# Attention steps in groups of four scores, two-bank maxima, a held GpSimd queue and re-placed norm rows in a transformer block

## The chip, the cores and the metric

The kernel runs on one core of one Trainium2 chip. The metric is device microseconds of that core for one execution. A kernel's time is the median of its runs. Engines are named as in the profile: PE (TensorE), DVE (VectorE), ACT (ScalarE), POOL (GpSimd), SP (SyncE); PEld is PE's loading of weights.

## The reference

One block with a conditioning vector: softmax attention with 32 heads of 16 dimensions over 2048 tokens, then a gated feed-forward part, in float32.

```python
mod = (silu(c) @ w_mod).reshape(1, 6, 1, 512); sa, ca, ga, sb, cb, gb = mod[:, 0..5]
h = layernorm(x) * (1 + ca) + sa                       # x: 1 x 2048 x 512
q, k, v = split_heads(h @ wqkv)                        # 32 heads of 16
p = softmax(q @ k.T * 16 ** -0.5)                      # 32 x 2048 x 2048
x = x + ga * (merge(p @ v) @ wo)
h = layernorm(x) * (1 + cb) + sb
x = x + gb * ((silu(h @ w_gate) * (h @ w_up)) @ w_down)    # 512 -> 1792 -> 512
```

## The kernel before

**Units and steps.** Attention is cut into 32 units of 4 heads by 512 queries. A unit takes 16 steps of 128 keys, so there are 512 steps. Eight units make a chunk of 512 tokens; there are four chunks, and the output projection and the feed-forward part of a chunk follow its attention, mixed into the attention of the next chunk.

**What a step issues.** For each of its four heads a pair of matmuls: `score` (L506) for the present step and `max_one` (L479) for the step 19 steps ahead, whose result only serves to find each query's maximum. The two use opposite halves of PE's rows and run side by side. ACT reads a score from its PSUM bank and writes its exponential (L508). DVE reduces the max matmul's bank to one maximum for each of 128 queries (L481). Then come the products with V (L521): two "halves" of a step, each of four matmuls of 256 columns; they may use a step's exponentials once the following step's four pairs have been issued. `pair_of` issues a pair, `pvs` the products with V, `close_unit` what follows a unit's last product (copy of the result `o` by ACT, L525; the softmax denominators go through DRAM and come back as `rb`; `out_c` multiplies on POOL and stores).

**Banks.** PSUM has eight banks of 512 columns. In steps without filler (`plain`) the max matmuls rotate over banks 0 to 3 (`four`), the scores over banks 4, 5 and 6 (`bank`), and the products with V accumulate in bank 7 (`single`). Every engine works its instructions in the order of issue; the whole order is written out by hand, and a matmul into a bank waits until the reader of that bank's last contents is done.

**Where steps are plain, where filled.** `plain(n)` runs n steps of attention alone, `filled` runs pairs with matmuls of the output projection or of the feed-forward part between them. `plain` takes the first 147 steps (the first chunk has nothing to mix in), then in each of the three chunks 12 steps while the chunk's rows are normed and transposed (`turned`, four of them, "tails"), 3 steps before the last `down` in two chunks, 21 steps at two chunk starts and 24 (`REST`) in the third: 255 of the 512 steps. In `plain` before, a group is three pairs (`WIN`) and then two, one, one, two halves of products (`HALVES`), so three steps make four groups.

**Unit ends.** Twelve steps into a unit the maxima of the next one are complete: `max_rows` reduces them on DVE (L486), PE transposes them (L491 to L493) into one of the score banks, ACT copies them to `mr` (L495), and SP's queue writes them into the rows of `qop` that the next unit's scores read (L497, `qop<-mr`).

**POOL.** During the first chunk POOL splits the weights into high and low parts (`split_weights`, three portions in each unit) and stores them to DRAM (`wo_dr`, `gu_dr`, `wd_dr`) through its own DMA queue. Nothing ties these portions to the attention's steps but POOL's order and `out_c`, which waits for `rb`. `begin` makes a chunk's object, loads its rows of x (`load_x2`) and its output weights (`load_wo`) through the same queue.

**The end.** After step 512 PE finishes the seven kept jobs of chunk 2 (`rest`), the last output projection, the norm of the last chunk's rows, their transposes, and the whole feed-forward part of chunk 3, with no attention beside it.

Of the kernel before, what the change touches and what calls it, by code (L numbers as in the profile page):

```python
# [39 lines left out]
WIN = 3  # L40
HALVES = (2, 1, 1, 2)
# [6 lines left out]
NORM = 9  # L48
# [53 lines left out]
def block_kernel(ctx, tc, x, wqkv, wo, w_gate, w_up, w_down, c, w_mod, out):  # L102
# [9 lines left out]
    banks = [ps.tile([P, CW], F32, name=f"bank{i}") for i in range(8)]  # L112
# [340 lines left out]
    posts = []  # L453
    n = 16 * NU
# [15 lines left out]
    def max_one(r):  # L470

        u, t = divmod(r // 4, 16)
        b, e = 1 - r % 4 // 2, r % 2
        s, qt, kc = t // 8, t // 2 % 4, t % 2 * 2 + e
        if u not in mx:
            mx[u] = pb.tile([P, 2, 2, 4, NC], F32, name="mx", tag="mx", bufs=3)
        rows = slice(64 * b, 64 * b + KR)
        pm = four("pm")
        nc.tensor.matmul(pm, qop[u][rows, s, qt * P:(qt + 1) * P], kop[u % 3][rows, s, kc * CW:(kc + 1) * CW],  # L479
                         start=True, stop=True)  # L480
        nc.vector.tensor_reduce(mx[u][:, b, s, qt, kc:kc + 1], pm, op=ALU.max, axis=AX.X)  # L481
# [281 lines left out]
    def gate_up(ch, f, outs, halves):  # L763
# [5 lines left out]
        def after():  # L769
            th = tmp("th")  # L770
            nc.scalar.activation(th, outs[0], AF.Tanh, scale=0.5)  # L771

            def later():
                q = tmp("q")
                nc.vector.scalar_tensor_tensor(q, th, 1.0, outs[0], op0=ALU.add, op1=ALU.mult)  # L775
                m32 = tmp("m32")
                nc.vector.tensor_mul(m32, outs[1], q)  # L777
                (nc.gpsimd.tensor_copy if halves else nc.scalar.copy)(mid[:, 0, :], m32)  # L778
                (nc.gpsimd if halves else nc.vector).tensor_sub(mid[:, 1, :], m32, mid[:, 0, :].bitcast(F32))  # L779
            posts.append(later)  # L780
# [25 lines left out]
    def begin(ci):  # L806
# [5 lines left out]
        ch.load_wo([as_wo(tile_gu()) for _ in range(NK // 2)])  # L812
# [20 lines left out]
    def close_unit(u, i):  # L833
        if u == NU - 1:
            res[u] = out_a(u, nc.scalar)
            return
        res[u] = out_a(u, nc.sync)
# [3 lines left out]
        if u % NG == NG - 1:  # L841
            at(i + 1, lambda: begin(u // NG))
# [9 lines left out]

    weights2 = split_weights()

    def after(i):
# [15 lines left out]
        if 0 <= i < UG and i % 16 in (1, 4, 7):  # L871
            next(weights2, None)
# [13 lines left out]
    done, ended, owed = 0, 0, 0  # L886
# [14 lines left out]
    def pvs(most, by_halves):  # L901

        nonlocal owed
        if by_halves:
            most, owed = most + owed, 0
        while most and halves and 4 * halves[0][0] + 8 <= done:
# [3 lines left out]
            if i % 16 == 15 and half:  # L910
                close_unit(i // 16, done // 4 - 1)
                if by_halves:
                    break
        if by_halves and most and halves and 4 * halves[0][0] + 8 <= done:
            owed = most
# [7 lines left out]
    def plain(steps, tails=()):  # L923

        nonlocal four, bank
        assert steps % WIN == 0 and done % 4 == 0
        four, bank = Turn(0, 1, 2, 3), Turn(4, 5, 6)
        for w in range(4 * steps // WIN):
            for _ in range(WIN):
                pair_of()  # L930
            if w >= 4 * steps // WIN - len(tails):
                tails[w - 4 * steps // WIN](four())
            pvs((HALVES[(w - 2) % 4] if done > 8 else 0) + (w == 4 * steps // WIN - 1), True)
            end_steps()

    def filled(places, work):
# [11 lines left out]
        pvs(6, False)  # L948
# [13 lines left out]
    for ci in range(last):  # L962
# [8 lines left out]
        plain(WIN, [lambda tp, k=k: ch.turned(tp, k) for k in range(NK)])  # L971
        if ci == last - 1:
            plain(REST)
        for _ in range(len(ch.jobs) - (KEEP if ci == last - 1 else 0)):
            job, args = ch.jobs.pop(0)
            if args == (NF // FG - 1, 0):
                plain(WIN)
# [8 lines left out]
    turns = chain([2, 3, 2, 0, 1, 3, 0], cycle([1, 2, 3, 0]))  # L986
# [12 lines left out]
    ch, chp = chunks[last], chunks[last - 1]  # L999
    rest = whole(chp, chp.jobs)  # L1000
# [6 lines left out]
    ch.load_x2(nc.scalar)  # L1007
# [8 lines left out]
    for t in range(4):  # L1016
        ch.normalize(t, True)
# [36 lines left out]
```

## Time and profile before

| | |
|---|---|
| median of 3 runs | 1947.17 us (1943.54 to 1949.21) |
| the profiled execution's own time | 1939.03 us |
| its span, first to last instruction | 1937.2 us |
| PE busy | 1891.8 us (98%) |
| DVE busy | 1551.5 us (80%) |
| ACT busy | 1256.0 us (65%) |
| POOL busy | 378.6 us (20%) |

A row of the profile's groups gives line, engine, operation, tiles as out<-in, shapes and count, then busy time in us and the mean ns of one, then the idle time before them and what ended it. A row of the timeline gives start and length in us, then engine, line and operation; an idle time that ended just there stands in brackets with its releaser. A row of the windows gives the stretch, its length, and each engine's busy time with the count of instructions, then the granted PE clock (1.00 is full), the DMA engines' busy share and GB/s; asked for one line, it counts that line alone. In the chain of waits a row gives start, length and what the chain passed through.

Since PE's records are pipelined (a matmul's record lasts longer than the time until the next may start), a PE that is 98% busy may still wait: the distance between starts tells its pace.

### The profile page before, as it was taken

How to read it: one execution, taken by the hardware profiler on the slowest of the kernel's cores; microseconds unless marked ns; L12 is line 12 of the kernel's file. 1: busy time of each engine (PE TensorE's matmuls, PEld its weight loads, DVE VectorE, ACT ScalarE, POOL GpSimd, SP SyncE). 2: the span in 40 equal slices, each digit the busy share in tenths (PEclk: the TensorE clock that was granted, in tenths of full speed). 3: DMA queues.
4: the chain of work that ended last, by engine and by line, in shares of the span. 5: the costliest groups of instructions: out<-in, count | busy, mean ns of one | idle time of the engine just before them, and what ended most of it. 6: DMA issues, size and time to landing. Idle time of an engine off the chain costs nothing.

```text
span 1937.2 us, 40750 instructions
## 1 busy us (share of the span) xinstructions
PE 1891.8 (98%) x16996; PEld 1152.4 (59%) x16996; DVE 1551.5 (80%) x2562; ACT 1256.0 (65%) x2333; POOL 378.6 (20%) x440
## 2 busy tenths in 40 slices
PE   7999999999999999999999999999999999999999
PEld 5766444444455666666555666666554466666787
DVE  5458999999899888888999888888999988831543
ACT  4222888888787666666777666666778866674211
POOL 3000435543223111111123101111123011121100
PEclk9999999999899999999999999999999999999999
DMA  8764666665453345443444334453532344243543
GB/s 286 274 218 121 185 179 183 194 198 150 141 110 72 103 114 142 138 118 85 133 95 101 100 125 118 122 136 75 153 84 54 97 97 138 111 140 110 222 194 109
DMA packets 79988, 267.60 MB, mean 138 GB/s; under 512 B 17364, under 2 KB 22484, under 8 KB 59124
## 3 DMA queue, kind: packets, MB, share of 16 engines
q1 hardware_dynamic: 64396, 200.22, 37.9%
q0 software_dynamic: 14192, 62.93, 9.4%
q8 instruction: 133, 2.18, 0.5%
q10 hardware_dynamic: 1216, 1.85, 0.3%
q14 instruction: 51, 0.42, 0.1%
HBM read 201.85 MB, written 62.13 MB: 136 GB/s over the span
## 4 chain that ended last, share of the span: by engine, by line
PE 88%; DVE 6%; ACT 3%; DMA 3%; issue 1%; SPq 0%; POOL 0%; ACTq 0%; DVEq 0%; POOLq 0%
PE bank L521 24%; PE bank L506 22%; PE bank L718 19%; PE bank L479 9%; PE bank L209 6%; PE bank L727 6%; DVE x L790 2%; DVE mx L481 2%; DMA qop<-mr 1%; PE bank L491 1%; DVE stt L743 1%; DMA v_flat<-in_A_x 0%; PE bank L703 0%; PE bank L162 0%; DMA wm_ab<-in_w_mod 0%
## 5 line engine op out<-in xcount | busy, mean ns | idle before, releaser
L481 DVE TENSOR_REDUCE mx<-bank 128x1 f32<-128x512 f32 x2048 | 1295.0, 682 | 168.3 <-PE bank L479 108.9
L506 PE MATMUL bank<-qop,kop 50*128 50x512 f32 x2048 | 751.1, 431 | 14.4 <-DMA qop<-mr 8.1
L479 PE MATMUL bank<-kop,qop 48*128 48x512 f32 x2048 | 759.7, 435 | 3.4 <-DVE mx L481 1.9
L506 PEld LDWEIGHTS bank<-qop,kop 50*128 50x128 f32 x2048 | 344.9, 185 | 322.2 <-issue 55.8
L479 PEld LDWEIGHTS bank<-kop,qop 48*128 48x128 f32 x2048 | 342.2, 185 | 29.5 <-DVE mx L481 10.4
L718 PE MATMUL bank<-act,wgu 64*128 64x512 f32 x1872 | 309.1, 394 | 1.5
L718 PEld LDWEIGHTS bank<-act,wgu 64*128 64x128 f32 x1872 | 199.8, 187 | 40.9 <-DVE x L790 9.0
L548 POOL TENSOR_TENSOR on<-o,rb 128x512 f32<-128x512 f32 x31 | 39.8, 1284 | 529.3 <-DMA rb<-d_dr 369.5
L718 PE MATMUL bank<-wd,mid 64*128 64x512 f32 x912 | 140.0, 396 | 1.7
L778 POOL CAST mid<-m 128x512 fp32r<-128x512 f32 x39 | 23.9, 613 | 469.7 <-DVE m L777 469.6
L718 PEld LDWEIGHTS bank<-wd,mid 64*128 64x128 f32 x912 | 92.0, 186 | 26.5 <-DVE x L790 11.0
L209 PE MATMUL bank<-hT,wqs 128*128 128x512 f32 x384 | 97.0, 404 | 3.9 <-DVE prt L369 2.4
L209 PEld LDWEIGHTS bank<-hT,wqs 128*128 128x128 f32 x384 | 71.5, 191 | 26.3 <-issue 5.9
L775 DVE SCALAR_TENSOR_TENSOR q<-th,bank 128x512 f32<-128x512 f32 x56 | 38.1, 680 | 55.8 <-ACT th L771 55.8
L771 ACT ACTIVATE th<-bank 128x512 f32<-128x512 f32 x56 | 33.4, 597 | 58.9 <-PE bank L727 58.5
L790 DVE TENSOR_TENSOR x<-bank,x 128x512 f32<-128x512 f32 x84 | 53.7, 680 | 21.0 <-PE bank L718 21.0
L369 DVE TENSOR_TENSOR prt<-bank,prt 128x512 fp32r<-128x512 f32 x32 | 21.9, 688 | 47.2 <-ACT prt L367 45.2
L367 ACT CAST prt<-bank 128x512 fp32r<-128x512 f32 x32 | 18.8, 586 | 60.5 <-PE bank L209 47.4
L777 DVE TENSOR_TENSOR m<-bank,q 128x512 f32<-128x512 f32 x56 | 38.7, 691 | 22.9 <-PE bank L727 19.2
L727 PE MATMUL bank<-wd,mid 128*128 128x512 f32 x216 | 52.8, 397 | 1.0 <-ACT mid L778 0.6
L779 POOL TENSOR_TENSOR mid<-m,mid 128x512 fp32r<-128x512 f32 x39 | 50.2, 1287 | 3.2
L718 PE MATMUL bank<-wgu,act 64*128 64x512 f32 x288 | 47.9, 395 | 0.1
(6279 smaller groups left out, 5124.5 us busy)
## 6 DMA issues: line engine op xcount, KB each, us to landing
wgu<-gu_dr SPq DMA_DIRECT2D x48, 1024.0 KB
kop<-kd SPq DMA_DIRECT2D x62, 768.0 KB
wd<-wd_dr SPq DMA_DIRECT2D x28, 1024.0 KB
gu_dr<-wgu POOLq DMA_DIRECT2D x14, 1024.0 KB, 4.1
qop<-qd SPq DMA_DIRECT2D x64, 192.0 KB
kd<-prt SPq DMA_DIRECT2D x16, 512.0 KB
qd<-prt SPq DMA_DIRECT2D x16, 512.0 KB
kop<-gu_dr SPq DMA_DIRECT2D x8, 1024.0 KB
```

The costliest lines, as they stand in the source:

```text
L209: nc.tensor.matmul(pt, lhs(a, k), rhs(b, k), start=(n == 0), stop=(n == 3 * nk - 1))
L479: nc.tensor.matmul(pm, qop[u][rows, s, qt * P:(qt + 1) * P], kop[u % 3][rows, s, kc * CW:(kc + 1) * CW], start=True, stop=True)
L481: nc.vector.tensor_reduce(mx[u][:, b, s, qt, kc:kc + 1], pm, op=ALU.max, axis=AX.X)
L506: nc.tensor.matmul(sp, kop[u % 3][rows, h // 2, kt * P:(kt + 1) * P], qop[u][rows, h // 2, :], start=True, stop=True)
L521: nc.tensor.matmul(pv[u][32 * h:32 * h + 32, cols], v_flat[:, e0:e0 + 32], p_[h][:, cols], start=(kt == 0 and half == 0), stop=(kt == 15), ...
L548: mul.tensor_mul(on, o, rb)
L718: nc.tensor.matmul(outs[e], lhs(e, a, k)[rows], rhs(b, k)[rows], start=(ph == 0 and j == 0), stop=(ph == 1 and j == z))
L727: nc.tensor.matmul(outs[e], lhs(e, a, k), rhs(b, k), start=(j == 0), stop=(j == z))
L775: nc.vector.scalar_tensor_tensor(q, th, 1.0, outs[0], op0=ALU.add, op1=ALU.mult)
L777: nc.vector.tensor_mul(m32, outs[1], q)
L779: (nc.gpsimd if halves else nc.vector).tensor_sub(mid[:, 1, :], m32, mid[:, 0, :].bitcast(F32))
L790: nc.vector.tensor_add(ch.x2[:, t, :], outs[e], ch.x2[:, t, :])
```

## The change

1. All eight banks become slices of one PSUM tile `psum`; the banks, their rotation and their waits stay tied to the slices.
2. In `plain` a group is one whole step: four pairs, then up to three halves of products (two are available in a steady row of steps). `WIN`, `HALVES` and the carrying over of owed halves are gone.
3. In `plain` one DVE instruction reduces two neighbouring banks (L485, output 128x2, input 128x2x512) after every second pair, in place of two of 128x512. `filled` steps keep the single reduce.
4. `tails` of `plain` take their bank from the score banks (`bank`) and no longer from the max banks, one per step (four steps, `NK`); the steps before them go from 9 to 8, so the 12 stay 12.
5. In units 0 to 6, `close_unit` queues a copy of one element of `o` to `pin` on POOL (L842), so that POOL goes no further before ACT has written `o`. The first portion of weights in a unit comes after step 2 and no longer after step 1.
6. The first chunk's `begin` moves from its end to step 3; its `load_wo` comes 6 steps after the close of its last unit, not 1, and so behind `out_c`.
7. At the end the last chunk's `load_x2` goes to POOL's queue, right after the last unit is closed, and no longer to ACT's queue behind the chain of `o`; two of its four rows are normed by POOL instead of ACT; its transposes use banks 6 and 7 instead of 4 and 5; the order of banks (`turns`) is changed to suit; and one split of a middle tile (chunk 2, f = 12) goes to POOL.

The core of the diff:

```diff
-WIN = 3
-HALVES = (2, 1, 1, 2)
-NORM = 9
+NORM = 8
-    banks = [ps.tile([P, CW], F32, name=f"bank{i}") for i in range(8)]
+    psum = ps.tile([P, 8, CW], F32, name="psum")
+    banks = [psum[:, i, :] for i in range(8)]
 ...
-        nc.vector.tensor_reduce(mx[u][:, b, s, qt, kc:kc + 1], pm, op=ALU.max, axis=AX.X)
+        if not wide:
+            nc.vector.tensor_reduce(mx[u][:, b, s, qt, kc:kc + 1], pm, op=ALU.max, axis=AX.X)
+        elif e:
+            two = psum[:, r % 4 - 1:r % 4 + 1, :]
+            nc.vector.tensor_reduce(mx[u][:, b, s, qt, kc - 1:kc + 1], two, op=ALU.max, axis=AX.X)
 ...
+        if u < NG - 1:
+            nc.gpsimd.tensor_copy(pin, o_[u][0:1, 0:1])
 ...
-            at(i + 1, lambda: begin(u // NG))
+            if u // NG:
+                at(i + 1, lambda: begin(u // NG))
+            at(i + (1 if u // NG else 6), lambda: chunks[u // NG].load_wo([...]))
 ...
+    at(3, lambda: begin(0))
 ...
     def plain(steps, tails=()):
-        four, bank = Turn(0, 1, 2, 3), Turn(4, 5, 6)
-        for w in range(4 * steps // WIN):
-            for _ in range(WIN):
+        four, bank, wide = Turn(0, 1, 2, 3), Turn(4, 5, 6), True
+        for w in range(steps):
+            for _ in range(4):
                 pair_of()
-            if w >= 4 * steps // WIN - len(tails):
-                tails[w - 4 * steps // WIN](four())
-            pvs((HALVES[(w - 2) % 4] if done > 8 else 0) + (w == 4 * steps // WIN - 1), True)
+            if w >= steps - len(tails):
+                tails[w - steps](bank())
+            pvs(3)
             end_steps()
 ...
+    ch.load_x2(nc.gpsimd)
 ...
-    ch.load_x2(nc.scalar)
 ...
-        ch.normalize(t, True)
+        ch.normalize(t, t < 2)
 ...
-            ch.turned(banks[4 + e], k + e, nc.vector if k else nc.gpsimd)
+            ch.turned(banks[6 + e], k + e, nc.vector if k else nc.gpsimd)
```

What PE has in its queue in a plain row of steps before (bank0 to bank3 take max matmuls, bank4 to bank6 scores, bank7 the products; `qop` and `kop` are a unit's queries and keys, `pt_` the exponentials):

```order
L506 MATMUL bank5_68<-qop_1098,kop1_961 128x512
L479 MATMUL bank0_63<-kop2_1417,qop_1422 128x512
L506 MATMUL bank6_69<-qop_1098,kop1_961 128x512
L479 MATMUL bank1_64<-kop2_1417,qop_1422 128x512
L506 MATMUL bank4_67<-qop_1098,kop1_961 128x512
L479 MATMUL bank2_65<-kop2_1417,qop_1422 128x512
L521 MATMUL bank7_70<-pt__2077,v_flat_88 32x256
L521 MATMUL bank7_70<-pt__2103,v_flat_88 32x256
L521 MATMUL bank7_70<-pt__2082,v_flat_88 32x256
L521 MATMUL bank7_70<-pt__2108,v_flat_88 32x256
L506 MATMUL bank5_68<-qop_1098,kop1_961 128x512
L479 MATMUL bank3_66<-kop2_1417,qop_1422 128x512
```

And at such a place now (the lines of `score` and of the products are 510 and 525 there, and all banks carry the name of the one tile; in the code a score still takes banks 4, 5 and 6 in turn, so the fourth score of a group takes the bank of the first):

```order
L510 MATMUL psum_63<-qop_957,kop0_80 128x512
L479 MATMUL psum_63<-kop1_954,qop_1092 128x512
L510 MATMUL psum_63<-qop_957,kop0_80 128x512
L479 MATMUL psum_63<-kop1_954,qop_1092 128x512
L510 MATMUL psum_63<-qop_957,kop0_80 128x512
L479 MATMUL psum_63<-kop1_954,qop_1092 128x512
L510 MATMUL psum_63<-qop_957,kop0_80 128x512
L479 MATMUL psum_63<-kop1_954,qop_1092 128x512
```

Between two visits to the same score bank there were products with V before; now a group's fourth score follows the first in the same bank with two other pairs between and no product.

POOL at the end of the first chunk before (`gu_dr`, `wd_dr` the stored weights, `x` the rows of x, `on` the multiplied result that waits for `rb`):

```order
L548 TENSOR_TENSOR on<-o,rb 128x512
L549 DMA o_dr<-on 128x512
L621 TENSOR_TENSOR mid<-mid,gb_bc 128x1024
L583 CAST wd<-mid 128x1024
L584 TENSOR_TENSOR wd<-mid,wd 128x1024
L587 DMA wd_dr<-wd 128x2048
L641 DMA x_5478<-in_A_x 128x4x512
L646 DMA wgu<-wo_dr 128x2048 x2
L548 TENSOR_TENSOR on<-o,rb 128x512
```

And now:

```order
L552 TENSOR_TENSOR on<-o,rb 128x512
L553 DMA o_dr<-on 128x512
L625 TENSOR_TENSOR mid<-mid,gb_bc 128x1024
L587 CAST wd<-mid 128x1024
L588 TENSOR_TENSOR wd<-mid,wd 128x1024
L591 DMA wd_dr<-wd 128x2048
L552 TENSOR_TENSOR on<-o,rb 128x512
L553 DMA o_dr<-on 128x512
L650 DMA wgu<-wo_dr 128x2048 x2
```

The load of x has left this place for step 3, and the two loads of output weights stand behind the last unit's multiplication, which waits for that unit's `rb`.

More of the change, by code (lines that the diff above doesn't have):

```diff
@@ L851, in before @@
             load_q(u + 2)
+    at(3, lambda: begin(0))
     weights2 = split_weights()
+    pin = pb.tile([1, 1], F32, name="pin", bufs=1)
     def after(i):
@@ L870, in after @@
             load_q(2)
[L871 removed]
+        if 0 <= i < UG and i % 16 in (2, 4, 7):
             next(weights2, None)
@@ L970, in block_kernel @@
         plain(NORM)
-        plain(WIN, [lambda tp, k=k: ch.turned(tp, k) for k in range(NK)])
+        plain(NK, [lambda tp, k=k: ch.turned(tp, k) for k in range(NK)])
         if ci == last - 1:
@@ L976, in block_kernel @@
             if args == (NF // FG - 1, 0):
-                plain(WIN)
+                plain(3)
             work = job(ch, *args, outs, True)
```

28 lines of the change are left out of this document (12 added, 16 removed).

## The prediction

> **What bounds the kernel now.** I read the page's first and fifth parts, then the windows of the plain stretches, then the timeline inside them, then the chain of waits where a stretch is longer than its pace explains.
>
> ```profile
> PE 1891.8 (98%) x16996; PEld 1152.4 (59%) x16996; DVE 1551.5 (80%) x2562; ACT 1256.0 (65%) x2333; POOL 378.6 (20%) x440
> ...
> L481 DVE TENSOR_REDUCE mx<-bank 128x1 f32<-128x512 f32 x2048 | 1295.0, 682 | 168.3 <-PE bank L479 108.9
> ```
>
> PE looks full everywhere, so the page does not say which engine paces a plain step. The change touches plain steps, so these are counted first: windows over the stretches of `plain`, asked for ACT's exponentials (L508) alone, four of which are a step (588 are 147 steps; a count can lack one).
>
> ```profile
> 189.71:563.42 373.71, 305.65 (x588) 0.98 0.61 169
> 592.28:625.96 33.68, 25.27 (x48) 1.00 0.20 43
> ...
> 940.47:992.47 52.00, 43.70 (x84) 1.00 0.52 142
> ...
> 1483.94:1543.22 59.28, 49.80 (x96) 1.00 0.34 71
> sum 652.67, ACT 530.98; mean ACT 59.00
> ```
>
> All 255 plain steps take 652.67 us, 2.56 each. In a quiet part the pace is DVE's:
>
> ```profile
> 440.55 21.54 DVE L481 TENSOR_REDUCE mx<-bank 128x1 f32<-128x512 f32 x36
> 462.01 0.21 DVE L486 TENSOR_REDUCE m<-mx 128x16 f32<-128x64 f32 x1
> ```
>
> Thirty-six reduces in 21.54 us without a gap are 0.598 us each, four of them 2.39 us: a quiet plain step. The rest, 652.67 - 255 x 2.39 = 43 us, sits at unit ends, tails and stalls. DVE is so the bound of plain steps, and halving its instructions looks like a gain. What would bound next is PE's own order, so I took its distances, start to start, from three pairs followed by two halves of products:
>
> ```profile
> 395.65 0.50 PE L506 MATMUL bank<-qop,kop 50*128 50x512 f32 x1
> ...
> 396.00 0.39 PE L506 MATMUL bank<-qop,kop 50*128 50x512 f32 x1
> ...
> 396.23 0.39 PE L506 MATMUL bank<-qop,kop 50*128 50x512 f32 x1
> ...
> 396.56 0.40 PE L521 MATMUL bank<-pt__3916,v_flat 128*32 128x256 f32 x1
> ...
> 397.56 0.50 PE L506 MATMUL bank<-qop,kop 50*128 50x512 f32 x1
> ```
>
> ```profile
> 396.19 0.60 ACT L508 ACTIVATE pt__3962<-bank 128x512 f32<-128x512 f32 x1
> 396.69 0.59 ACT L508 ACTIVATE pt__3967<-bank 128x512 f32<-128x512 f32 x1
> 397.16 0.60 ACT L508 ACTIVATE pt__3972<-bank 128x512 f32<-128x512 f32 x1
> ```
>
> First pair to second 0.35, second to third 0.23, two halves with both switches 1.00. The first score's exponential starts 0.54 after the score and takes 0.60; later ones follow at 0.47 to 0.50. Three scores, three banks: none waits in its own group.
>
> **The pace of the new group.** The fourth score takes the bank of the first, so it waits for the exponential of a score of its own group, and the products stand behind it in PE's queue. The trace holds this very case once: the last four scores of all rotate over three banks with no filler and no max matmul.
>
> ```profile
> 1766.65 0.73 PE L506 MATMUL bank<-qop,kop 50*128 50x512 f32 x3 [0.23 <-ACT pt__20527 L508]
> 1767.83 0.50 PE L506 MATMUL bank<-qop,kop 50*128 50x512 f32 x1 [0.45 <-ACT pt__20542 L508]
> 1768.26 0.40 PE L521 MATMUL bank<-pt__20504,v_flat 128*32 128x256 f32 x1
> ...
> 1767.18 0.60 ACT L508 ACTIVATE pt__20542<-bank 128x512 f32<-128x512 f32 x1 [0.59 <-PE bank L506]
> ```
>
> Three scores start at 1766.65, the exponential of the first at 1767.18, it ends at 1767.78, the fourth score goes at 1767.83, the products at 1768.26: 1.61 us from first score to products. With 1.00 for two halves and the switch back, the loop is 2.61 us, and it closes: the next group's first score stands behind these products. The other demands are smaller. DVE: 0.68 us for 512 elements and 0.21 for 64 give 1.04 ns per element, so 1024 cost 0.598 + 0.53 = 1.13 a piece, 2.26 a step (bounds: 1.07, no fixed part at all, and 1.36, two records end to end). ACT: four at 0.48, 1.92. The max matmuls add nothing: the second reduce begins about 1.9 after the first score, ends by 3.12, and the third pair that needs its banks comes at 2.61 + 0.58 = 3.19. Up to 1.30 a reduce stays hidden behind the loop, so what the wider reduce saves has no taker. I take 2.61 (bounds 2.55, the fourth score's pair as cheap as a warm one, and 2.72, two reduces of 1.36). 255 steps: 665.6 us.
>
> **Unit ends.** One step with the transposes of the maxima, and the lone transposes of a tail:
>
> ```profile
> 383.58:387.01 3.43, 2.66 (x6) 1.00 0.58 168
> ...
> 616.85 0.66 PE L703 MATMUL bank<-ident,mid 128*128 128x128 f32 x4
> ```
>
> The step costs 3.43 - 2.39 = 1.04 more. In the new group PE idles 1.18 - 0.81 = 0.37 before the fourth score, and the transposes, which stand after the first pair, fall into that: 0.67 is left (bounds 0.3 and 1.04). Of the 255 steps 18 hold one: 12 us.
>
> **Tails.** Four per chunk, twelve in all. Each now holds a score bank: its transposes wait for the second exponential (0.54 + 0.47 + 0.60 + 0.05 = 1.66 after the first score, against 1.61 without) and take 0.66. I take 0.7 each (bounds 0.5 and 1.3, if ACT's copy of that bank delays the next group): 8 us. NORM 8 + 4 keeps the count of steps. The first step has no products yet and saves 1. New sum of the plain stretches: 665.6 + 12 + 8 - 1 = 685, against 652.67: **32 us more**.
>
> **The hold and the moved loads.** The first stretch has 373.71 - 147 x 2.39 = 22 us over pace, 9 of it unit ends. Most of the rest is one place:
>
> ```profile
> 497.67 0.77 POOL L641 DMA_DIRECT2D x<-in_A_x  x1
> 498.44 1.06 POOL L646 DMA_DIRECT2D wgu<-wo_dr  x2
> ...
> 503.77 6.97 DMA qop<-mr
> ...
> 505.00:510.00 5.00, 1.32 (x18) 0.43 (x8) 2.43 (x4) 1.88 (x4) 0.00 (x0) 0.94 0.91 375
> 510.00:515.00 5.00, 4.12 (x24) 1.74 (x24) 1.36 (x3) 1.30 (x3) 0.00 (x0) 0.50 0.02 7
> ...
> 504.71:523.88 19.17, 8.47 (x18) 0.64 0.26 106
> ```
>
> POOL ran ahead of the attention and issued three loads just before the write of `mr`; that took 6.97 us, PE stood still, and its clock fell to 0.50. Four steps took 19.17 instead of 9.6. Both edits, `begin` at step 3 and `load_wo` behind `out_c`, take the loads from there, so these 9.6 and some 3 of smaller stalls go. My 685 already holds none of these 12.5; if the hold fails, they come back. The hold itself I cost at nothing:
>
> ```profile
> POOL on L548 <- DMA rb<-d_dr: 369.5, 20, 37.2
> ```
>
> POOL already waits once a unit for `rb`; now it waits at `pin` first, with the same work behind it. Queued behind are weight portions and `out_c`; nobody needs the weights before step 155, or `on` before the chunk's projection at step 147, some 30 us after the last portion. If that cover went, PE would wait at step 147 by what is late, at most a portion of about 6 us (part of the range). The later `load_wo` has the eleven steps to 147, also covered.
>
> **The end.**
>
> ```profile
> 1784.37 9.05 DMA v_flat<-in_A_x
> 1793.51 1.29 DVE v_flat L739 x2
> ...
> 1792.27 0.69 DVE L779 TENSOR_TENSOR mid<-m,mid 128x512 fp32r<-128x512 f32 x1 [0.69 <-ACT mid L778]
> 1802.01 2.93 ACT L695 ACTIVATE v_flat<-v_flat,rs,rs 128x512 f32<-128x512 f32 x4 [9.28 <-DVE rs L691]
> 1806.92 1.94 PE L703 MATMUL bank<-ident,v_flat 128*128 128x128 f32 x8 [3.08 <-DVE x L790]
> ...
> L698 POOL TENSOR_SCALAR mid<-x,rs,rs 128x512 f32<-128x512 f32 x12 | 9.1, 769 | 0.3
> ```
>
> The earlier load of x frees the additions at 1793.51, but DVE is at L779 until 1792.96: 0.55 won. Two rows on POOL (2 x 0.77) beside two on ACT save 1.4 of 2.93. Banks 6 and 7 no longer wait for L790. So PE's idle 3.08 before the transposes goes nearly whole: 3 us less (bounds 0, if the load of x slows the small transfers of `o`, and 4). The middle tile split on POOL is ready before its `down`: nothing.
>
> **Sum.** 32 - 3 = 29 us. The profiled execution took 1939.03, so 1968; the median of the runs stands 0.42% above it, so **1976 us**, 1.5% slower.
>
> **Rivals.**
>
> *The wait for the fourth score is not paid* (faster). If ACT answered sooner or PE passed the products ahead, the pace would be set by the loop through DVE's banks over two steps: reduce end, third and fourth pair (0.07 + 0.23), products 1.33, second pair 0.35 + 0.44, two reduces 1.13 + 1.21, together 4.76, 2.38 a step. Plain stretches: 255 x 2.38 + 19 = 626, 27 less, with the end 30: 1916 us. It decides from a pace of 2.48 on. The lone group at 1766.65 speaks against it. The Trainium skill, VectorE: DVE Perf Modes, section on the TRN2 errata, says that a fixed latency is paid once per instruction, so that few large tiles beat many small ones; by that alone the change is a gain on DVE. The trace agrees on the fixed part (0.21 for 64 elements, 0.68 for 512), but not that DVE sets the new pace.
>
> *The gains elsewhere cancel it* (no change): pace 2.50 and all stalls gone, about 1947.
>
> *A two-bank reduce costs two records or more* (1.36): DVE paces at 2.72, 28 us on top: 2004. No row shows such a reduce; the slope between 64 and 512 elements speaks against it.
>
> *PE's clock drops* because PE now idles 0.37 in every step. In the stall the clock fell to 0.50 after some 4 us of idling, and at 0.50 a step's four passes of products (4 x 0.22 between 396.56 and the switch) would take twice as long, 3.5 a step: 255 x 0.9 = 230, so 2200. The plain windows with PE's small waits stand at 1.00 throughout, which speaks against it. The Trainium skill, TensorE: Matmul & The Clock Gate, section on a second HAM failure mode, tells of micro-idles between groups of matmuls, as PE cycles through PSUM banks, that throttle the clock; no run here shows it for gaps this short.
>
> **How the numbers follow.** Forecast 0.80, clock 0.02, dear reduce 0.05, cancelled 0.06, wait not paid 0.07. The forecast's own range: pace -15 to +18, unit ends and tails -8 to +14, stalls that stay 0 to +12, end -1 to +3, not all at once: 1956 to 2000. To hold 8 in 10 with the cases beside it: 1950 to 2003. What can be told from no change here is about 0.3% (6 us). Slower 0.88 (forecast, clock, dear reduce, a little of the cancelled), within 0.3% 0.05, faster 0.07.
>
> **What would show it.** In the plain windows: 2.6 us per four exponentials; DVE with gaps, its releaser PE; the fourth score of a group with an idle time released by ACT; two-bank reduces near 1.2 us. At the end of the first chunk no stall of 7 us and the clock at 1.00. Before the last transposes no idle 3 us. Wrong would be: DVE without gaps at 2.3, or plain stretches under 652 us.

## The result and the profile after

The changed kernel takes 1979.4 us (median of 4 runs, 1976.8 to 1980.6) against 1946.9 for the one before (4 runs, 1943.5 to 1949.2): a ratio of 1.017, interval 1.0154 to 1.0185. The forecast was 1976, slower. The profiled execution spans 1975.0 us, 37.8 more than that of before.

First the page of the changed kernel: busy time of PE and DVE, then the group of two-bank maxima, with busy time, mean ns of one, and the idle time before them.

```profile
PE 1912.4 (97%) x16996; PEld 1182.2 (60%) x16996; DVE 1535.2 (78%) x2051; ACT 1254.9 (64%) x2330; POOL 383.4 (19%) x452
...
L485 DVE TENSOR_REDUCE mx<-psum 128x2 f32<-128x1024 f32 x510 | 599.0, 1219 | 80.8 <-PE psum L479 50.7
```

DVE has 511 instructions and 16 us less to do, and idles 80.8 us before its new ones, most of it for want of PE: the saved time found no taker.

The windows over the plain stretches of the changed kernel, exponentials alone (now L512; four are a step, and a window may count the one that closes it):

```profile
191.58:584.06 392.48, 305.58 (x588) 1.00 0.56 161
...
964.53:1020.89 56.36, 43.70 (x84) 1.00 0.48 131
...
sum 692.66, ACT 530.62; mean ACT 58.96
```

Before, the sum was 652.67: **40 us more** for the same 255 steps, in every window. The clock is 1.00 in each of them, so it isn't PE's clock. One quiet step of it, on the timeline of PE and then of ACT; below them a stretch of DVE a few steps on:

```profile
367.93 0.50 PE L510 MATMUL psum<-qop,kop 50*128 50x512 f32 x1
...
368.27 0.40 PE L510 MATMUL psum<-qop,kop 50*128 50x512 f32 x1
...
368.51 0.39 PE L510 MATMUL psum<-qop,kop 50*128 50x512 f32 x1
...
369.12 0.50 PE L510 MATMUL psum<-qop,kop 50*128 50x512 f32 x1 [0.21 <-ACT pt__3325 L512]
...
369.55 0.40 PE L525 MATMUL psum<-pt__3298,v_flat 128*32 128x256 f32 x1
...
370.55 0.50 PE L510 MATMUL psum<-qop,kop 50*128 50x512 f32 x1
```

```profile
368.47 0.60 ACT L512 ACTIVATE pt__3325<-psum 128x512 f32<-128x512 f32 x1 [0.55 <-PE psum L479]
```

```profile
402.19 3.48 DVE L485 TENSOR_REDUCE mx<-psum 128x2 f32<-128x1024 f32 x3
```

Three scores start within 0.6 us; the exponential of the first runs from 368.47 to 369.07, and the fourth score goes at 369.12, released by it. The products follow at 369.55 and the next group at 370.55: 370.55 - 367.93 = 2.62. Quiet steps are 2.61 to 2.62; the first two after a unit end are up to 0.14 longer. Three two-bank reduces in 3.48 us with the last record of 1.22 make (3.48 - 1.22) / 2 = 1.13 from one to the next.

The end of the first chunk, where before one write of `mr` took 6.97 us and the clock fell to 0.50 (all engines, then clock, DMA share, GB/s):

```profile
530.00:535.00 5.00, 4.85 (x52) 2.40 (x47) 4.74 (x6) 3.99 (x9) 0.00 (x0) 1.00 0.03 6
```

No stall and no fall of the clock. And the end, where PE idled 3.08 us before the last transposes; the group of these transposes, and ACT's two norm rows that were four:

```profile
L707 PE MATMUL psum<-ident,v_flat 128*128 128x128 f32 x16 | 2.1, 272 | 0.0
```

```profile
1843.92 1.52 ACT L699 ACTIVATE v_flat<-v_flat,rs,rs 128x512 f32<-128x512 f32 x2 [8.66 <-DVE rs L695]
```

From the last step's first exponential to the end it is 164.8 us, before 170.1. So the difference of the spans closes: +40.0 in the plain steps, +1.1 in filled ones, +1.9 before the first exponential, -5.2 at the end.

### The profile page after: what moved, and what is told of

Its sections match the earlier page's. It is cut to its first block, busy times and chain, and to the rows that moved or that the text cites. A ratio compares the mean times of both kernels' runs of the same rounds, so it can differ in the third digit from the quotient of the medians.

```text
span 1975.0 us, 40244 instructions
## 1 busy us (share of the span) xinstructions
PE 1912.4 (97%) x16996; PEld 1182.2 (60%) x16996; DVE 1535.2 (78%) x2051; ACT 1254.9 (64%) x2330; POOL 383.4 (19%) x452
## 4 chain that ended last, share of the span: by engine, by line
PE 80%; DVE 9%; ACT 8%; DMA 2%; issue 1%; SPq 0%; ACTq 0%; DVEq 0%
PE psum L525 22%; PE psum L510 19%; PE psum L722 17%; PE psum L731 7%; PE psum L208 6%; PE psum L479 6%; DVE mx L485 3%; DVE mx L482 2%; DVE x L795 2%; DMA wgu<-gu_dr 1%; ACT o L529 1%; PE psum L764 1%; PE psum L495 1%; DVE stt L747 0%; PE psum L161 0%
## 5 line engine op out<-in xcount | busy, mean ns | idle before, releaser
L510 PE MATMUL psum<-qop,kop 50*128 50x512 f32 x2048 | 767.0, 433 | 29.1 <-ACT pt__20033 L512 0.5
L479 PE MATMUL psum<-kop,qop 48*128 48x512 f32 x2048 | 786.5, 443 | 7.5 <-DVE mx L485 3.7
L482 DVE TENSOR_REDUCE mx<-psum 128x1 f32<-128x512 f32 x1028 | 677.4, 687 | 145.2 <-PE psum L479 73.2
L485 DVE TENSOR_REDUCE mx<-psum 128x2 f32<-128x1024 f32 x510 | 599.0, 1219 | 80.8 <-PE psum L479 50.7
L510 PEld LDWEIGHTS psum<-qop,kop 50*128 50x128 f32 x2048 | 343.3, 184 | 341.2 <-issue 38.2
L479 PEld LDWEIGHTS psum<-kop,qop 48*128 48x128 f32 x2048 | 339.2, 184 | 46.6 <-DVE mx L485 14.5
L722 PE MATMUL psum<-act,wgu 64*128 64x512 f32 x1872 | 310.1, 395 | 2.9 <-DMA wgu<-gu_dr 0.9
L722 PEld LDWEIGHTS psum<-act,wgu 64*128 64x128 f32 x1872 | 200.5, 187 | 41.6 <-DVE x L795 9.0
L722 PE MATMUL psum<-wd,mid 64*128 64x512 f32 x912 | 140.1, 396 | 1.7
L208 PE MATMUL psum<-hT,wqs 128*128 128x512 f32 x384 | 98.4, 408 | 3.9 <-DVE prt L368 2.4
```

The source lines that it names most:

```text
L208: nc.tensor.matmul(pt, lhs(a, k), rhs(b, k), start=(n == 0), stop=(n == 3 * nk - 1))
L485: nc.vector.tensor_reduce(mx[u][:, b, s, qt, kc - 1:kc + 1], two, op=ALU.max, axis=AX.X)
L510: nc.tensor.matmul(sp, kop[u % 3][rows, h // 2, kt * P:(kt + 1) * P], qop[u][rows, h // 2, :], start=True, stop=True)
L722: nc.tensor.matmul(outs[e], lhs(e, a, k)[rows], rhs(b, k)[rows], start=(ph == 0 and j == 0), stop=(ph == 1 and j == z))
```

## The experiments

Numbers of a step are distances between every fourth exponential in the trace; "147 steps" is the first plain stretch (373.7 us before, 392.5 after). Each median has its ratio to the runs of before beside it in time, whose medians were 1943.2 to 1946.9 us.

| kernel | quiet step, us | 147 steps, us | median, us |
|---|---|---|---|
| before | 2.39 | 373.7 | 1947 |
| after | 2.61 | 392.5 | 1979.4 |
| e2: single maxima | 2.61 | 390.1 | 1974.4 |
| e12: half of the maxima, 3 score banks | 2.61 | 389.8 | 1967.2 (one run) |
| e13: half of the maxima, 4 score banks | 2.04 | 318.8 | 1850.4 (one run) |
| e8: single maxima over 3 banks, 4 score banks | 2.74 | 413.1 | 2007.3 |
| e3: groups of three, two-bank maxima | 2.79 | 415.1 | 2010.6 |
| e14: groups of three, half of the maxima two-bank, no hold | 2.44 | 383.3 | 1950.0 |
| e1: groups of three, single maxima | 2.39 | 401.2 | 1960.3 |
| e11: e1 without the hold | 2.39 | 373.2 | 1931.3 |
| e9: groups of two | 2.46 | 403.0 | 1986.8 |
| e10: e9 without the hold | 2.46 | 378.3 | 1952.8 |
| e5: after without the hold | 2.61 | 394.6 | 1977.8 |
| e4: e5 with the loads of before | 2.61 | 395.3 | 1980.5 |

### What sets the pace of a group of four

**e2: one maximum per bank.**

```diff
-        four, bank, wide = Turn(0, 1, 2, 3), Turn(4, 5, 6), True
+        four, bank, wide = Turn(0, 1, 2, 3), Turn(4, 5, 6), False
```

> After with one maximum per bank in place of one over two; the group of one step and all else stay. Theory (the fourth score waits for the exponential of the first, so the DVE's instruction doesn't set the pace): four maxima are 2.39 us, less than the 2.61 of the loop, so the step stays 2.61 and the time within 1974 to 1986 us. Rival 1 (the two-bank maximum sets the pace, by its length of 1.22 us or by freeing two banks at once): the step falls to 2.4 to 2.5 us and the time to 1920 to 1950 us. Rival 2 (the two-bank form did save something): 1990 us or more.

1974.4 us (ratio to before 1.015, 1.0118 to 1.0178), and the step is the same. PE and ACT of a quiet step:

```profile
402.01 0.50 PE L510 MATMUL psum<-qop,kop 50*128 50x512 f32 x1
...
403.19 0.49 PE L510 MATMUL psum<-qop,kop 50*128 50x512 f32 x1 [0.22 <-ACT pt__3896 L512]
...
404.63 0.50 PE L510 MATMUL psum<-qop,kop 50*128 50x512 f32 x1
```

```profile
402.55 0.60 ACT L512 ACTIVATE pt__3896<-psum 128x512 f32<-128x512 f32 x1 [0.55 <-PE psum L510]
```

Here, too, the profile names the releaser: the fourth score waited for `pt__3896`, the first exponential of its own group. 404.63 - 402.01 = 2.62. The two-bank instruction neither sets this pace nor pays.

**e12 and e13: half of the maxima left out, three or four banks for scores.**

```diff
+        if wide and e:
+            return
         pm = four("pm")
...
-        nc.scalar.activation(p_, sp, AF.Exp, scale=SCALE)
+        nc.scalar.activation(p_, sp, AF.Exp, scale=SCALE / 8)
...
-        four, bank, wide = Turn(0, 1, 2, 3), Turn(4, 5, 6), True
+        four, bank, wide = Turn(0, 1, 2), Turn(4, 5, 6), True        # e12
+        four, bank, wide = Turn(0, 1, 2), Turn(3, 4, 5, 6), True     # e13
```

> After without the hold, and in the plain steps with two of the four maxima of a step left out (matmul and reduction; the exponentials are scaled down so that they stay finite), the two that are left over three banks, the four scores over three banks as in after. The DVE then has half of its work and no maximum can wait for a bank. Theory (the fourth score's wait for the first exponential of its group is the whole of what a step takes over TensorE's own work): the step stays 2.58 to 2.65 us and the time 1960 to 1985 us. Rival (the DVE or the banks of the maxima have a share in the 2.61 us): 2.5 us or less, 1950 us or less.

> The kernel with two maxima a step left out, and the bank that they leave free given to the scores: four scores over four banks. Theory: no score waits for an exponential of its own group, and what is left is TensorE's own work of four pairs and one step of products, worked out from the steps of the cut kernel (2.46 us with two changes between pairs and products, some 0.1 to 0.15 us each way): 2.13 to 2.30 us a step, so 255 x 0.31 to 0.48 = 79 to 122 us less than the same kernel with three banks for scores. Rival (a group of one step is slow by itself): within 20 us of it.

The exponentials in one window of 100 us, first of e12, then of e13:

```profile
250.00:350.00 100.00, 78.34 (x152) 1.00 0.65 175
```

```profile
250.00:350.00 100.00, 93.70 (x184) 1.00 0.75 209
```

With half of the maxima left DVE is busy for 49.7 of the 100 us in e12, and the step is still 2.61. With one bank more for the scores and nothing else changed it is 1.96 and 2.12 in turn, 2.04 on average, and the whole kernel is 117 us shorter, within the 79 to 122 expected (the quiet step came out below its range of 2.13 to 2.30, but unit ends gain less than quiet steps). So the wait for the fourth score's bank is shown to make at least 0.57 us of the step. That the 2.04 left are PE's own work is not shown: in e13 ACT is busy with exponentials for 93.70 of 100 us, and in its quiet steps it works almost without a gap (8 exponentials in 4.08 us), so there ACT sets the pace. Nor is it the work of a full step, which has two max matmuls more. From the rows of before, four pairs and a step of products without a wait would take some 0.35 + 0.23 + 0.23 + 0.33 + 1.00 = 2.14 us, an estimate.

**e8: the fourth bank taken from the maxima.** All work is done, four banks for scores, three for single maxima.

```diff
-        four, bank, wide = Turn(0, 1, 2, 3), Turn(4, 5, 6), True
+        four, bank, wide = Turn(0, 1, 2), Turn(3, 4, 5, 6), False
```

> After with one bank taken from the maxima and given to the scores (four banks for scores, three for maxima with one instruction per bank); the group of one step and all else stay. Theory (the wait of the fourth score for the first exponential of its group makes the 2.61 us): with a bank of its own the fourth score waits for nothing of its group, the pace falls to that of four single maxima, 4 x 0.598 = 2.39 us, or a little over (to 2.47), so 255 x 0.15 to 0.23 = 38 to 58 us less than after: 1920 to 1941 us. Rival (a group of one step is slow in itself, because pairs and products come in lumps): the step stays at 2.6 us or more and the time at 1975 us or more, since the maxima have one bank less.

2007.3 us (1.0318, 1.0294 to 1.0341), step 2.74: the forecast of 2.39 to 2.47 fell. The rival's number came out, and of its two reasons not the lumps but the bank that the maxima lose:

```profile
401.82 0.50 PE L479 MATMUL psum<-kop,qop 48*128 48x512 f32 x1
...
403.13 0.50 PE L479 MATMUL psum<-kop,qop 48*128 48x512 f32 x1
```

```profile
402.38 2.48 DVE L482 TENSOR_REDUCE mx<-psum 128x1 f32<-128x512 f32 x4 [0.25 <-PE psum L479]
```

Now the fourth *maximum* wants the bank of the first of its own group, whose reduction (0.68 long) starts at 402.38 and ends at 403.06; PE goes on at 403.13, 1.31 after the group's start, where after has 1.18. The 0.13 is the 2.74 - 2.61. The forecast went by DVE's rate (4 x 0.598), not by its answer to the first of four. A group of four over three banks pays the same kind of wait whichever engine frees them.

### What the two-bank maximum does in groups of three

**e3: groups of three pairs, two-bank maxima, the hold and the end of after.** Besides the lines shown, halves of products are counted out as in before.

```diff
         four, bank, wide = Turn(0, 1, 2, 3), Turn(4, 5, 6), True
-        for w in range(steps):
-            for _ in range(4):
+        for w in range(4 * steps // WIN):
+            for _ in range(WIN):
                 pair_of()
...
-            pvs(3)
+            pvs((HALVES[(w - 2) % 4] if done > 8 else 0) + (w == 4 * steps // WIN - 1), True)
```

> After with groups of three pairs and half steps of products as before had them, but with the maximum over two banks kept, and the hold and the end edits. Theory (only the group of four scores costs): in groups of three no score waits for an exponential of its own group, the DVE needs 2 x 1.13 = 2.26 us a step, so a step takes 2.28 to 2.39 us and the time is 1900 to 1932 us, below both kernels. Rival (the two-bank maximum frees its banks in pairs and too late, whatever the groups): the step is 2.5 us or more and the time 1955 us or more.

2010.6 us (1.033, 1.0309 to 1.0351): the theory fell, the rival stands. Steps are 3.0, 3.0 and 2.37 in turn. DVE and PE:

```profile
381.41 3.49 DVE L487 TENSOR_REDUCE mx<-psum 128x2 f32<-128x1024 f32 x3 [0.76 <-PE psum L481]
```

```profile
382.29 0.50 PE L512 MATMUL psum<-qop,kop 50*128 50x512 f32 x1
382.68 0.50 PE L481 MATMUL psum<-kop,qop 48*128 48x512 f32 x1
...
383.81 0.50 PE L481 MATMUL psum<-kop,qop 48*128 48x512 f32 x1 [0.16 <-DVE mx L487]
```

The reduction of banks 0 and 1 runs from 381.41 to 382.63; the maximum that wants bank 0 goes at 382.68, 0.39 after the score it should run beside. The one at 383.81 waits for the next reduction, which ends at 383.76. A two-bank instruction starts when its second bank is full and frees both when it ends, so the first bank is away for 1.22 us and the time between the two matmuls, against 0.68 with single ones.

**e14: two-bank only where one group of three fills both banks.** It runs without the hold, so it is compared with e11 below.

```diff
-            for _ in range(WIN):
+            for j in range(WIN):
+                wide = (WIN * w + j) % 12 not in (2, 3, 8, 9)
                 pair_of()
```

> Groups of three pairs without the hold (1931 us with single maxima, DVE bound at 2.39 us a step), with a two-bank maximum only where both banks are filled by the same group of three: four two-bank and four single ones in three steps. Theory (in groups of three it was the two-bank maxima across a stretch of products that kept banks; DVE then needs (4 x 1.13 + 4 x 0.60) / 3 = 2.31 us a step): 2.31 to 2.37 us a step, 1905 to 1927 us. Rival (any two-bank maximum keeps its first bank too long for groups of three, since the group after it wants that bank before the longer instruction ends): 2.45 us a step or more, 1945 us or more.

1950.0 us (1.0035, 1.002 to 1.0049), 19 more than e11. DVE over one period of three steps:

```profile
440.19 2.34 DVE L487 TENSOR_REDUCE mx<-psum 128x2 f32<-128x1024 f32 x2
...
445.16 1.22 DVE L487 TENSOR_REDUCE mx<-psum 128x2 f32<-128x1024 f32 x1 [0.30 <-PE psum L481]
...
447.51 2.35 DVE L487 TENSOR_REDUCE mx<-psum 128x2 f32<-128x1024 f32 x2
```

```profile
441.46 0.50 PE L481 MATMUL psum<-kop,qop 48*128 48x512 f32 x1
```

A period is 447.51 - 440.19 = 7.32, 2.44 a step: the 6.92 of the sum, and 0.4 around the one gap where PE comes late with a second bank. PE was held before that: the maximum at 441.46 wants the first bank of the reduction that began at 440.19 and took 1.22, and goes 0.05 after its end. The gap takes back what the longer instruction saves, and more: 10 us in the 147 steps. That is the rival's account, with the step at its edge.

### What the hold costs

**e1: the groups and single maxima of before, the rest of after.** This asks whether anything but the plain loop costs time. The edit is that of e3, and single maxima, with the tails' banks as in before:

```diff
-        four, bank, wide = Turn(0, 1, 2, 3), Turn(4, 5, 6), True
+        four, bank, wide = Turn(0, 1, 2, 3), Turn(4, 5, 6), False
...
-                tails[w - steps](bank())
+                tails[w - 4 * steps // WIN](four())
```

> After with the order of the plain steps of before: groups of three pairs, half steps of products, one maximum per bank, the extra operations ahead of each group as before; the hold at unit ends, the moved loads and the end edits stay. Theory (the loss is the group of four scores over three banks, the other edits gain or cost nothing): a plain step takes 2.39 us again where after has 2.61, the stall of some 12 us at the end of the first chunk stays away and the end stays 5 us shorter, so 1947 - 12 - 5 = 1930 us, within 1924 to 1940. Rival (the hold, the moved loads or the one tile that now holds all banks costs the time): the steps stay near 2.6 us and the time is 1960 us or more.

1960.3 us (1.007, 1.0053 to 1.0088): outside the theory's range, at the rival's edge. The quiet step is 2.39 as expected, but seven unit ends of the first chunk have steps of 5 to 7 us. PE's waits between 190 and 584 us (total, times, longest), one of them on the chain, and the window behind it:

```profile
PE psum L481 <- DMA qop<-qd: 18.1, 7, 3.1
```

```profile
340.37 16.22 DMA qop<-qd
...
356.68 0.47 PE psum L481
```

```profile
357.20:360.60 3.40, 3.40 (x23) 1.42 (x22) 1.91 (x4) 1.14 (x3) 0.00 (x0) 0.50 0.38 149
```

The load of Q that SP issues in the seventh step of a unit takes 16 to 17 us and comes 2 to 3 late; behind this wait the clock is 0.50 for 3.4 us, and at five others of the seven for 3.4 to 10.2. The waits are 18.1 us of what the hold costs (below), and the slow clock goes with the rest. Here are SP's queue in e1 and POOL's copy to `pin` and its next store of weights:

```profile
335.05 0.34 SPq L543 DMA_DIRECT2D d_dr<-dn  x1
337.08 0.55 SPq L548 DMA_DIRECT2D rb<-d_dr  x1
337.73 1.91 SPq L405 DMA_DIRECT2D kop<-kd  x2
339.69 1.50 SPq L405 DMA_DIRECT2D qop<-qd  x2
```

```profile
327.63 0.18 POOL L844 COPY pin<-o 1x1 f32<-1x1 f32 x1 [16.57 <-ACT o L531]
...
338.61 0.59 POOL L593 DMA_DIRECT2D gu_dr<-wgu  x1 [0.30 <-POOL wgu L590]
```

Between its wait at `pin` and the next wait for `rb`, POOL now loads and stores weights just while SP's small transfers of `dn` and the loads of K and Q are under way.

**e11: e1 without the hold.**

```diff
-        if u < NG - 1:
-            nc.gpsimd.tensor_copy(pin, o_[u][0:1, 0:1])
```

> The groups of three pairs of the earlier run, without the hold of GpSimd. There the step was 2.39 us again, but at seven unit ends of the first chunk TensorE waited 2 to 5 us for a load of Q, with a low clock behind it, and the time was 1960 us where 1930 was expected. Theory (the hold bunches GpSimd's loads of weights so that they collide with SP's load of Q, and only a slow step leaves time for that): without the hold the waits go, the end stays 5 us shorter than in before, and of the 12 us stall at the end of the first chunk some or all comes back: 1924 to 1944 us. Rival (the waits come from the moved loads of the first chunk or from the common tile of banks): 1955 us or more.

1931.3 us (8 runs; 0.993, 0.9903 to 0.9957), inside the theory's range and the fastest kernel of the study that does all of the work. Its quiet step is 2.39 with all banks in one tile, so the one tile does not slow the step. No wait for a load of Q is left. POOL's last store before SP's loads in the same unit, and SP's queue:

```profile
316.50 0.59 POOL L593 DMA_DIRECT2D gu_dr<-wgu  x1 [0.30 <-POOL wgu L590]
```

```profile
326.60 0.34 SPq L543 DMA_DIRECT2D d_dr<-dn  x1
328.05 0.55 SPq L548 DMA_DIRECT2D rb<-d_dr  x1
328.70 0.90 SPq L405 DMA_DIRECT2D kop<-kd  x2
329.65 1.41 SPq L405 DMA_DIRECT2D qop<-qd  x2
```

Without the hold POOL works its portions ahead: its last store goes 13 us before the load of Q, in e1 1 us before it. From `d_dr` to the load of Q SP takes 3.05 us, in e1 4.64: the small transfer that `rb` waits for takes 0.6 longer there, the issue of the loads of K 1.0 longer. So the load of Q starts 1.6 us later; beside POOL's stores it also lands 16.9 us after its issue (356.59 against 339.69), in e11 15.6 (345.21 against 329.65). The two make 2.9 us, and PE's wait in this unit is 2.5. That the hold costs is shown; that it does so through POOL's stores is read from these times, since no run moves the stores alone. From the first exponential to the last step's, e1 takes 1604.9 us and e11 1577.9: the hold costs 27 us. Of e11's 13 us against before, the profiles show 6 at the end (163.9 against 170.1), and the other 7 they don't show. The first stretch is the same 373 us: the stall at the chunk's end is gone (31.0 us for 13 steps, 40.8 before), but slow first steps take back 5 of it (5.2 us for the third, at a clock of 0.50), and slow steps at a few unit ends most of the rest, where PE waits for the write of `mr` (5.1 us in four waits).

**e5: after without the hold.** The same two lines taken out.

> After without the small copy that holds GpSimd at unit ends; all else stays. Theory (with a step of 2.61 us there is time for the loads of K and Q either way, so the hold neither costs nor gains): 1975 to 1983 us, and no wait for a load of Q. Rival 1 (the hold is what took the 7 us stall and the 5 us beside it out of the end of the first chunk): 1987 us or more. Rival 2 (the hold costs, as it seems to in groups of three pairs): 1970 us or less.

1977.8 us (1.0173, 1.0132 to 1.0214), no wait for a load of Q and no stall like that of before (its longest wait for the write of `mr` is 0.7 us). The hold is worth nothing at a step of 2.61, for or against.

**e4: e5 with `begin(0)` and the load of wo where before has them.**

```diff
-            if u // NG:
-                at(i + 1, lambda: begin(u // NG))
-            at(i + (1 if u // NG else 6), lambda: ...load_wo(...))
+            at(i + 1, lambda: begin(u // NG))
+            at(i + 1, lambda: ...load_wo(...))
-    at(3, lambda: begin(0))
```

> After without the hold and with the first chunk's beginning and its loads of wo back at the step after the last unit's end, as in before. Theory (the moved loads take the stall of some 12 us out of the end of the first chunk; the hold alone was shown to change nothing): the stall comes back, 1985 to 1993 us. Rival (the slower step alone gives the loads time): 1974 to 1982 us.

1980.5 us (1.0183, 1.015 to 1.0216): the rival's. PE's wait for the write of `mr` there, POOL's last loads before it and the write, and the window:

```profile
PE psum L510 <- DMA qop<-mr: 0.9, 1, 0.9
```

```profile
522.44 1.07 POOL L650 DMA_DIRECT2D wgu<-wo_dr  x2
...
530.83 4.38 DMA qop<-mr
```

```profile
530.00:535.00 5.00, 4.41 (x46) 1.89 (x44) 4.62 (x4) 3.86 (x8) 0.00 (x0) 1.00 0.75 308
```

The loads are there again (308 GB/s where after moved 6), the wait is 0.9 us and the clock stays. The write starts 7.3 us after the loads are issued and takes 4.38; in before it started 4.3 us after them (503.77 against 499.50) and took 6.97. In this kernel the old place of the loads does no harm to speak of; in e11, at 2.39, the moved loads are there and the stall is gone too. Both keep the first portion of weights after step 2, which no run here takes back.

**e9 and e10: the step cut in two, with and without the hold.** Two pairs, half of the products, two pairs, the other half; two-bank maxima.

```diff
-        for w in range(steps):
-            for _ in range(4):
+        for w in range(2 * steps):
+            for _ in range(2):
                 pair_of()
...
-            pvs(3)
+            pvs(3 if w == 2 * steps - 1 else 1 + (open_ > 2))
```

> After with the step cut in two: two scores and two maxima, half of the products, two scores and two maxima, the other half; two-bank maxima and the hold stay. Theory (the fourth score waits because the products stand behind all four; and a two-bank maximum costs nothing if the half step between gives it time): the fourth score comes 0.5 us later than the first exponential ends, so the step falls to the DVE's 2 x 1.13 = 2.26 us or little more (to 2.40), but with this pace the hold lets TensorE wait for Q at unit ends, as in groups of three pairs (some 30 us): 1905 to 1950 us. Rival (a two-bank maximum frees its banks too late in any order, as in groups of three): a step of 2.55 us or more, 1965 us or more.

> The kernel with the step cut in two, without the hold of GpSimd. Theory (as for the one with it, and the hold is what makes TensorE wait for Q): a step of 2.26 to 2.40 us, so 255 x 0.21 to 0.35 = 54 to 89 us less than after, less what comes back of the stall at the end of the first chunk (up to 12): 1890 to 1937 us, and 10 to 40 us less than the same kernel with the hold. Rival (the pace alone makes the waits for Q): within 6 us of the same kernel with the hold.

e9 took 1986.8 us (1.0212, 1.0141 to 1.0283) and e10 1952.8 (1.0039, 1.0013 to 1.0065): both above their ranges, and the difference of 34 within the 10 to 40 expected. Not all of it is the hold's. Between the first and the last step the profiled executions take 1627.3 and 1594.0 us; 25 us of these 33 lie in the first 147 steps, where POOL is held, and 10 in the third chunk, where it isn't and where PE's clock in e9 is 0.50 for 24 us (1060 to 1084). The step is 2.46 where I had 2.26 to 2.40. PE in e10:

```profile
402.87 0.50 PE L510 MATMUL psum<-qop,kop 50*128 50x512 f32 x1
...
403.54 0.40 PE L525 MATMUL psum<-pt__3754,v_flat 128*32 128x256 f32 x1
...
404.11 0.50 PE L510 MATMUL psum<-qop,kop 50*128 50x512 f32 x1
```

No score waits; two pairs take 0.67 and half of the products 0.57, 1.24 each time. PE pays for the second change between pairs and products, some 0.3 us over the 2.14 estimated above for a whole step without a wait. The trace of before had the price: there, too, a single half takes 0.57.

```profile
398.46 0.40 PE L521 MATMUL bank<-pt__3943,v_flat 128*32 128x256 f32 x1
...
399.03 0.49 PE L506 MATMUL bank<-qop,kop 50*128 50x512 f32 x1
```

With 0.35 and 0.33 for the pairs that gives 2 x (0.35 + 0.33 + 0.57) = 2.50 a step; the forecast went by DVE's 2.26.

## Why the prediction was right, and where not

**The pace.** Forecast 2.61 by the loop score, exponential, fourth score, products; measured 2.61 to 2.62 in every stretch. e2 shows that it is nothing of the two-bank instruction, e12 that it is nothing of DVE's work, and e13 that the wait goes with a fourth bank. The lone group of four in the last step of before's trace held the answer.

**The two-bank maximum.** Forecast 1.13 from one to the next and 1.21 long, measured 1.13 and 1.219; "what the wider reduce saves has no taker" is shown by e2. The Trainium skill, VectorE: DVE Perf Modes, section on the TRN2 errata, has one large tile beat many small ones, for operations that read from SBUF. The trace agrees as far as DVE goes, here with reads from PSUM (2 x 0.598 - 1.13 = 0.07 us saved a pair), but in groups of three the larger instruction lost time (e3, e14), by how long it keeps its banks.

**The plain steps.** Forecast 685 us, measured 692.7. Unit ends cost 0.75 us more than quiet steps and not 0.67, tails 0.66 and not 0.70. One term had the wrong sign: the first two steps cost 1.4 us over the pace (2.14 and 4.45), where I took 1 off. One was missing: once in each of the three times when a chunk's rows are normed, DVE's norm chain stands between two reductions and PE waits for a bank:

```profile
616.93 0.49 PE L479 MATMUL psum<-kop,qop 48*128 48x512 f32 x1 [1.13 <-DVE mx L485]
```

1.1 us each time, 3.4 in all. First steps, unit ends, tails and norm chain make 2.4 + 1.4 - 0.5 + 3.4 = 6.7 of the 7.7; the rest is the pace, nearer to 2.615 than to 2.61.

**The stalls.** "These 9.6 and some 3 of smaller stalls go" was right in the sum, and its cause was not needed. The step that failed is "if the hold fails, they come back": without the hold (e5) and with the old loads too (e4) they don't come back. What the traces show in its place is more time between the loads and the write of `mr` (7.3 us in e4, 4.3 in before).

**The hold.** "The hold itself I cost at nothing" is right for this kernel and was right for too small a reason. I named who needs the weights and `on`, and left out who shares the DMA engines with POOL's stores: SP's load of Q. At 2.39 and 2.46 us a step the hold costs 28 and 25 us in the first 147 steps (e1 with e11, e9 with e10); the new step of 2.61 covers it. The Trainium skill, DMA: Bandwidth & Descriptors, section on issuing engines not being separate DMA queues, says that transfers of different engines run on the same 16 DMA engines and interleave; e1, where SP's loads of 1920 KB run beside POOL's store of 1024 KB, agrees in direction: the load of Q lands after 16.9 us there and after 15.6 without such a store.

**The end.** Forecast -3 (bounds 0 and -4), measured -5.2: PE's idle time of 3.08 us before the transposes went whole, as worked out. The other 2 us lie just behind it. In before the clock was 0.50 from 1806.5 to 1809.9, and the first eight transposes took 1.94 us where they now take 1.03; and a wait of 0.64 us for ACT's split of a middle tile is gone, a term that the forecast put at nothing.

**Luck in the number.** Forecast 1976, measured 1979.4, but the profiled execution was forecast at 1968 and took 1976.8. Of the 9 us that the sum lacked, 5 were made up by chance: 8 us were added for the distance from the profiled execution to the median, which is 2.6 here.

**The rivals.** "The wait for the fourth score is not paid" would have taken a bank that isn't there: e13 shows what it is worth. "The gains elsewhere cancel it" fell with the pace, and "A two-bank reduce costs two records or more" with the 1.13 us. "PE's clock drops" did not come in the plain windows (1.00 with a wait of 0.4 us in each step; in before the first of them stood at 0.98, not at 1.00 like the others). It did at the start: a window in the second step of after.

```profile
196.00:198.00 2.00, 2.00 (x20) 0.86 (x14) 0.92 (x1) 0.00 (x0) 0.00 (x0) 0.50 1.04 195
```

The 1.9 us before the first exponential are no part of the change that I can name: over the kernels here, with the same order of work ahead of it, it stands between 187.9 and 191.6.

## What to carry to other kernels

Count the buffers that one burst of an in-order engine fills before it turns to other work: a burst of four over three banks makes the fourth wait for the answer to the first, and all that stands behind it in the queue, whether ACT or DVE answers. A wider instruction saves its engine little and keeps its buffers longer; ask for both, and for who would use the time saved. A wait that costs nothing now may be covered by the slowness that one wants to remove: test it again with the faster loop, and look at what shares the DMA engines with the transfers that it moves.

## What the runs showed of the hardware that I had not expected

- Going from pairs to products and back twice in a step, not once, costs PE some 0.3 us (2.46 in e10 against 2.14, an estimate from rows of before): two halves apart take 2 x 0.57, two together 1.00, and the rest is in the pairs.
- At six of e1's seven waits of 2 to 3 us PE's granted clock was 0.50 for 3.4 to 10.2 us, and it was 0.50 in the first steps of several kernels after waits of about 0.2 us each (3.4 us in after from 195, 13.7 in e11 from 192.5, 20.5 in e8 from 194), but 1.00 in before at the same place. What decides this stays open.
